# Two halves of the heads for the first unit of a gated-linear-attention and maxout kernel, with q and k of a head pair laid side by side and a new planned order

## The chip, the cores and the metric

The kernel runs on one core of a Trainium2 chip. The metric is the device time of the whole program in microseconds; the kernel before has a median of 138.03 us over 5 runs (137.97 to 138.18).

## What is computed

The attention part is a recurrence over 768 time steps for each of 4 batches and 8 heads of width 48; its output feeds a maxout block.

```python
for t in range(S):                                   # S = 768, D = 48
    state = alpha[:, :, t, :, None] * state + einsum('bhd,bhe->bhde', k[:, :, t], v[:, :, t])
    y[:, :, t] = einsum('bhd,bhde->bhe', q[:, :, t], state)
x = y.transpose(0, 2, 1, 3).reshape(B * S, H * D)    # 3072 x 384
h1, h2 = x @ w1, x @ w2                              # 384 x 1024 each
out = maximum(h1, h2) @ w_out                        # 1024 x 384
```

All inputs and the output are float32; the kernel computes with 16-bit operands and 32-bit sums.

## The kernel before: how the work is tiled and ordered

**Units and chunks.** The 3072 rows are cut into 12 units of 256 time steps (a batch and one of three positions in it), and each unit into two chunks of 128. `gla(u)` does the attention of unit u, `moe(u)` its maxout. Units 0, 1 and 2 (the tuple `TWO`) hold two neighbouring time steps in each partition, so their loads have longer runs; the branch for them is called `by2` in the code.

**One unit of attention.** ScalarE takes the logarithm of alpha (L481), TensorE sums it along time (L503 for the first three units, L492 for the others), and ScalarE takes the exponentials of the sums with both signs: `em` (L530) and, in place in the bank, the factor for q (L532). `prep(i)` then multiplies k by `em` into `kn` (L573) and q by the factor into `qn` (L575), transposes both on TensorE (L583, four head pairs each into one bank), and copies the transposed pair out: into `qu` for the first three units (L588), into `qk` for the others (L593). `chunk(a)` makes P, the products of transposed k and q (L676); VectorE multiplies P by a triangular mask into `pt` (L698); TensorE adds up the output from `pt` and v (L710) and from the carried state and q (L707); ScalarE copies it to `yc` (L718); TensorE transposes it (L724) and VectorE copies the result to `xt` (L732, L735). The carried state goes through k times v (L604 or L647), a sum `tm` (L659, L661, L663) and a scaled copy `sb` on GpSimd (L634). GpSimd or VectorE also lays v out as 16 bits (`vx`, L556; the other half rows by ScalarE, L560).

**The maxout.** max(h1, h2) is written as x·w2 + relu(x·(w1 − w2)). So the kernel needs w1 − w2 in four pieces of 256 columns (`w12`, a VectorE subtraction, L460), w_out in 16 bits in four pieces (`wo16`, L465), and the product w2·w_out (`w2o`): w2 is cast (L432), transposed (L440), copied (L444) and multiplied by `wo16` (L450, 24 matmuls, six for each piece of w_out). `moe(u)` then has eight half-pairs: four products `hp` with one piece of `w12` each (L765, six matmuls), each followed by a relu on ScalarE (L776), and two output sums `op` (L796) that begin with the three matmuls on `w2o` and go on through the four pieces in order. ScalarE copies them out (L804) and issues the store (L812).

**What sets the order.** Nothing is ordered by the program text alone. Every step is entered with `add(engine, function, duration, reads, writes, key)`; a list scheduler (`Plan.schedule`) plays the engines forward with these durations and, on each engine, picks the ready step with the smallest key. Keys are 10·u plus an offset: 0 to 4.5 inside `gla(u)`, `KEY_M` and more inside `moe(u)`, `KEY_W`, `KEY_W12` and `KEY_WO` for the weights. The dictionary `PRI` shifts keys of single steps. The engines' instruction streams are then written in the planned order and each engine runs its own stream in order. Where the plan leaves TensorE idle in its first 40 us, `busy` puts matmuls on a constant tile there (L471). The first loads are issued by SyncE in the order of `HEAD`, in which `a0` is alpha of unit 0 and so on, `w20` to `w22` are the row blocks of w2, `w10` to `w13` the column pieces of w1, and `wo0` to `wo3` the pieces of w_out.

The lines that set the engine of single steps are these:

```python
KEY_W12 = 8; KEY_W = 3; KEY_WO = 21; KEY_M = 20
WT_ACT = (0,)       # w2T copies on ScalarE, the others on VectorE
WO_ACT = (2, 3)     # casts of w_out pieces on ScalarE, the others on GpSimd
TM_ACT = 2          # units whose first tm goes through ScalarE
QU_ACT = (1,)       # chunks whose qu copy is on ScalarE
KN_DVE = (0,); VX_DVE = (0,)   # chunks whose kn, vx are on VectorE, the others on GpSimd
HEAD = 'a0 a1 k0 q0 v0 q1 k1 w20 w22 v1 w21 wo0 wo1 wo2 w13 w10 wo3 w11 w12'
```

Of the kernel before, what the change touches and what calls it, by code (L numbers as in the profile page):

```python
# [7 lines left out]
FP16 = mybir.dt.float16  # L8
# [177 lines left out]

KEY_W12 = 8
KEY_W = 3
KEY_WO = 21
KEY_M = 20  # L190
CAPS = {'g': 6, 'm': 5, 'w': 3}
W12_POOL = ()
WT_ACT = (0,)
WO_ACT = (2, 3)
RELU_DVE = 99
TM_ACT = 2
X_LAST = 0
# [3 lines left out]
TWO = (0, 1, 2)  # L201
MERGE = 3
COMBO = 99
JOIN_CS = -2
JOIN_PP = -50
CS_UP = 2
RING = 3
# [3 lines left out]
XT_ACT = ()  # L211
QU_ACT = (1,)
KN_DVE = (0,)
VX_DVE = (0,)
PRI = {'PE:op.1.1.0@1': 10, 'PE:op.0.0.0@0': 15.0, 'PE:op.1.0.0@1': 3, 'PE:op.0.1.0@0': 4.5, 'DVE:tm.4.1@3': -33.5, "POOL:('vx', 2).1@2": -16.5, 'PE:hp.1.1@1': -3.0, 'PE:cs.4.0@4': -10, 'POOL:kn.1@6': -5, 'POOL:sb.0.0@4': 12, 'PE:hp.3.3@3': 1.5, 'ACT:qu.0.1@0': -13.5, 'PE:hp.4.1@4': 5.0, 'DVE:pt.1.1@5': 5, 'PE:pp.0.1.0@0': -15, 'DVE:pt.0.0@0': 9, 'PE:y.5.0@5': 10.5, 'PE:hp.5.1@5': 13.5, 'DVE:tm.2.1@3': -9, 'ACT:cs.7.0@7': 5, 'PE:op.4.1.0@4': 9, 'DVE:tm.2.1@4': -11, 'PE:y.0.0@0': 5, 'DVE:pt.0.1@3': 10, 'PE:cs.2.0@2': -9, 'DVE:tm.3.1@5': 9, 'ACT:cs.7.1@7': -5, 'PE:hp.2.3@2': -3, 'PE:pp.1.0.0@1': 3}
HEAD = 'a0 a1 k0 q0 v0 q1 k1 w20 w22 v1 w21 wo0 wo1 wo2 w13 w10 wo3 w11 w12'


@with_exitstack
def kernel(  # L220
# [53 lines left out]
    VX = sbt("vx", [128, 3, H, D], FP16, max(1, len(TWO)))  # L274
    QU = sbt("qu", [128, 2, 2, HP, 2, 64], FP16, 2)
    w2f, w1f = (LD[i].rearrange("p a x -> p (a x)").rearrange("p (s f) -> p s f", s=ND) for i in (4, 5))
# [18 lines left out]
    def two(t):  # L295
        return t.rearrange("p (h r d) -> p r h d", r=2, h=H)

    P = Plan()
# [78 lines left out]
    for i in range(RING):  # L377
        add("DVE", lambda i=i: nc.vector.memset(KN[i][:, :, D:64], 0.0), 0.17, writes=[("kn", i)], key=-6)
        add("DVE", lambda i=i: nc.vector.memset(QN[i][:, :, D:64], 0.0), 0.17, writes=[("qn", i)], key=-5)
    for i in range(2):  # L380
# [76 lines left out]
    def weights(g):  # L457
        fs = slice(256 * g, 256 * g + 256)
        eng, ns = ("POOL", nc.gpsimd) if g in W12_POOL else ("DVE", nc.vector)
        add(eng, lambda: ns.tensor_sub(out=w12[:, :, fs], in0=w1f[:, :, fs], in1=w2f[:, :, fs]),  # L460
            1.9 if g in W12_POOL else 0.95, reads=[("w1f", g), *(("w2f", ds) for ds in range(ND))],
            writes=[("w12", g)], key=KEY_W12)
        on = g in WO_ACT
        cp = nc.scalar.copy if on else nc.gpsimd.tensor_copy
        add("ACT" if on else "POOL", lambda: cp(  # L465
            out=wo16[:, 2 * g : 2 * g + 2, :], in_=wof[:, 2 * g : 2 * g + 2, :]),
            0.73 if on else 0.9, reads=[("wof", g)], writes=[("wo16", g)], key=KEY_W)

# [69 lines left out]
    def gla(u):  # L538
        P.u = u
        n, by2 = u % NLD, u in TWO  # L540
        k0 = 10 * u
        de, cp = DE[u % 8], u // B
# [21 lines left out]
        def prep(i):  # L564
# [7 lines left out]
            on, ns = ("DVE", nc.vector) if ci in KN_DVE else ("POOL", nc.gpsimd)  # L572
            add(on, lambda: ns.tensor_mul(out=kn[:, :, 0:D], in0=kin, in1=EM[m3]),  # L573
                0.55 if on == "DVE" else 0.97, reads=[*rk, ("em", m3)], writes=[("kn", m3)], key=kk)
            add("DVE", lambda: nc.vector.tensor_mul(out=qn[:, :, 0:D], in0=qin, in1=csv(u, i)),  # L575
                0.5, reads=[*rq, ("cs", u, i)], writes=[("qn", m3)], key=kk)
            tp = ("tp", u, i)
            P.ps(tp, 1, "g")
            for w, (src, key) in enumerate(((qn, ("qn", m3)), (kn, ("kn", m3)))):
                def e_tp(w=w, src=src):  # L580
                    t = b16(tp, 1024).rearrange("p (w j c) -> p w j c", w=2, j=HP)
                    for j in range(HP):
                        nc.tensor.transpose(t[:, w, j, :], pm(src[:, 2 * j : 2 * j + 2, :]), ident)  # L583
                add("PE", e_tp, 0.222, reads=[key, "ident"], writes=[tp], key=kk)
            if by2:
                on = ci in QU_ACT
                cp = nc.scalar.copy if on else nc.vector.tensor_copy
                add("ACT" if on else "DVE", lambda: cp(  # L588
                    out=qu[:, :, :, :, i, :].rearrange("p a w j c -> p (w j) a c"),
                    in_=b16(tp, 1024).rearrange("p (y a c) -> p y a c", a=2, c=64)),  # L590
                    1.0 if on else 0.65, reads=[tp], writes=[("qu", TWO.index(u) % 2, i)], key=kk)
            else:
                add("DVE", lambda: nc.vector.tensor_copy(  # L593
# [16 lines left out]
        def chunk(a):  # L610
# [7 lines left out]
            if by2:  # L618
                qt = [qu[:, a, w].rearrange("p j r c -> p j (r c)") for w in range(2)]
                rqk, vc, rv, um, ru = [("qu", TWO.index(u) % 2, 0), ("qu", TWO.index(u) % 2, 1)], vx[:, 2 * a], [(vk, x) for x in range(4)], u2, "u2"  # L620
            else:
# [16 lines left out]
            if more:  # L638
                if by2:
                    if a == 0:  # L640
                        P.ps(("kv", u, 1), 1, "g")
                        add("PE", kv2, 0.35, reads=[("kn", (2 * u) % RING), ("kn", (2 * u + 1) % RING), (vk, 0), (vk, 1)],
                            writes=[("kv", u, 0), ("kv", u, 1)], key=kk + 0.1, tiled=True)
                else:
                    def e_kv():
                        for j in range(HP):
# [3 lines left out]
                            )  # L650
                    add("PE", e_kv, 0.168, reads=[("kn", m3), ("vc", m4)], writes=[kvp], key=kk + 0.1)
                tmi = P.tm_next(u % B)
# [16 lines left out]

            def e_p(which):  # L670
                for w in which:
                    qt, pp, _ = qts[w]
                    for j in range(HP):
                        for e in range(2):
# [3 lines left out]
            if u < MERGE:  # L678
                add("PE", lambda: e_p((a,)), 0.215, reads=rqk, writes=pp, key=kk, tiled=True, join=kk + JOIN_PP)
            elif a == 0:  # L680
# [15 lines left out]
            uv = um.rearrange("p r c -> p (r c)") if by2 else um  # L696
            for e in range(2):
                add("DVE", lambda e=e: nc.vector.tensor_mul(  # L698
                    out=pt[:, e], in0=b32(pp[e], 512).rearrange("p (j c) -> p j c", j=HP),
                    in1=uv.unsqueeze(1).to_broadcast([128, HP, C])),  # L700
                    0.6, reads=[pp[e], ru], writes=[("pt", m3, e)], key=kk)

            def e_y():
# [10 lines left out]
            add("PE", e_y, 0.378 if has else 0.21,  # L714
                reads=[*rqk, ("pt", m3, 0), ("pt", m3, 1), *rv] + ([("sb", m4, 0), ("sb", m4, 1)] if has else []),
                writes=[yp], key=kk)
# [173 lines left out]
```

## Time and profile before

| What | Value |
|---|---|
| median of 5 runs | 138.03 us |
| the profiled execution's own time | 138.18 us |
| its span in the profile | 136.5 us, so 1.68 us lie around the span |
| TensorE busy (PE) | 131.7 us, 96% |
| VectorE (DVE), ScalarE (ACT), GpSimd (POOL) busy | 90.8, 91.1, 65.1 us |
| TensorE on the constant tile (L471) | 122 matmuls, 10.9 us busy, all before 18.8 us |
| granted TensorE clock | 1.0 in every stretch |

How to read it: PE is TensorE's matmuls and PEld its weight loads, which run beside them. Matmuls are pipelined, so a row's mean (273 ns for a 256-column product) is longer than the distance from one to the next; the chain of work that ended last shows the distances. Times in the views count from the start of the span.

### The profile page before, as it was taken

The page shows a single profiled execution, that of the slowest core. Times are in us where ns is not written, and L with a number is a line of the kernel's source. Part 1 is how long each engine was busy: PE and PEld are TensorE (multiplying, and loading weights), DVE is VectorE, ACT ScalarE, POOL GpSimd, SP SyncE. Part 2 cuts the span into 40 slices and gives each one's busy share as a digit, 9 for nine tenths or more (in the row PEclk, how much of TensorE's full clock was granted, in tenths as well). Part 3 has the DMA queues.
Part 4 walks back from the last instruction along what each step waited for, and adds up shares of the span by engine and source line. Part 5 has one row for each costly group of instructions (what it writes and reads, how often), then busy time and mean ns, then how long its engine had stood idle before and what let it go on. Part 6 is the DMA issues. An engine that isn't in the chain of part 4 may idle for free.

```text
span 136.5 us, 4240 instructions
## 1 busy us (share of the span) xinstructions
PE 131.7 (96%) x1669; PEld 102.2 (75%) x1669; DVE 90.8 (67%) x201; ACT 91.1 (67%) x189; POOL 65.1 (48%) x126
## 2 busy tenths in 40 slices
PE   6999999999999999999999999999999999999990
PEld 6898876777668777777877777777777778777870
DVE  4579897823899778967789479566758657572000
ACT  3697785899856956865846667568749468264640
POOL 7453974007594384470780773743747619300000
PEclk9999999999999999999999999999999999999999
DMA  3999999999999999979999989999979130030202
GB/s 93 323 325 389 388 371 356 294 250 261 212 218 258 265 233 196 313 154 221 296 185 248 252 202 231 207 214 285 222 172 237 37 115 0 5 115 0 102 30 104
DMA packets 84179, 28.58 MB, mean 209 GB/s; under 512 B 78400, under 2 KB 83392, under 8 KB 84160
## 3 DMA queue, kind: packets, MB, share of 16 engines
q1 hardware_dynamic: 81120, 23.60, 71.7%
q10 hardware_dynamic: 3040, 4.72, 9.5%
q8 instruction: 13, 0.21, 0.6%
q14 instruction: 6, 0.05, 0.1%
HBM read 23.59 MB, written 4.72 MB: 207 GB/s over the span
## 4 chain that ended last, share of the span: by engine, by line
PE 81%; SPq 8%; DMA 6%; ACT 1%; issue 1%; ACTq 0%
PE pb L796 31%; PE pb L765 23%; PE pb L583 7%; DMA ld<-in_moe_w_out_dram 6%; SPq L393 5%; PE pb L676 4%; SPq L421 3%; PE pb L710 3%; PE pb L724 3%; PE pb L707 2%; PE pb L492 2%; PE pb L450 2%; PE pb L647 2%; PE pb L525 1%; ACT wo L465 1%
## 5 line engine op out<-in xcount | busy, mean ns | idle before, releaser
L573 POOL TENSOR_TENSOR kn<-ld,em 128x384 f16<-128x384 f32 x23 | 22.7, 1001 | 35.5 <-ACT em L530 22.0
L796 PE MATMUL pb<-wo,gt 128*128 128x384 f16 (+2 forms) x200 | 39.2, 319 | 0.0
L765 PE MATMUL pb<-xt,w 128*128 128x256 f16 x288 | 35.6, 272 | 0.0
L698 DVE TENSOR_TENSOR pt<-pb,u 128x512 f16<-128x512 f32 x48 | 30.1, 683 | 6.2 <-PE pb L676 5.7
L776 ACT ACTIVATE gt<-pb 128x512 f16<-128x512 f32 x48 | 28.3, 599 | 8.4 <-PE pb L765 7.5
L765 PEld LDWEIGHTS <-w 128*128 128x128 f16 x288 | 27.0, 98 | 4.4 <-issue 0.6
L634 POOL TENSOR_TENSOR sb<-tm,dd 64x192 f16<-64x192 f32 x40 | 20.3, 506 | 11.3 <-DVE tm L659 5.1
L796 PEld LDWEIGHTS <-gt 128*128 128x128 f16 x200 | 17.4, 97 | 8.2 <-issue 0.3
L804 ACT COPY os<-pb 128x384 f32<-128x384 f32 (+2 forms) x25 | 11.7, 467 | 16.7 <-PE pb L796 16.7
L593 DVE COPY qk<-pb 128x1024 f16<-128x1024 f16 x18 | 12.4, 689 | 7.2 <-PE pb L583 7.1
L575 DVE TENSOR_TENSOR qn<-ld,pb 128x384 f16<-128x384 f32 x24 | 12.6, 548 | 6.9 <-ACT pb L532 4.9
L796 PE MATMUL pb<-w2o,xt 128*128 128x384 f16 (+2 forms) x75 | 15.8, 319 | 0.0
L718 ACT CAST yc<-pb 128x384 f16<-128x384 f32 x24 | 11.7, 489 | 5.4 <-PE pb L710 5.4
L530 ACT ACTIVATE em<-pb 128x384 f32<-128x384 f32 x24 | 11.2, 489 | 3.9 <-PE pb L492 2.6
L659 DVE TENSOR_TENSOR tm<-pb,sb 64x192 f32<-64x192 f32 x32 | 11.3, 353 | 1.0 <-PE pb L647 0.2
L471 PE MATMUL pb<-wsrc 128*128 128x128 f16 x122 | 10.9, 251 | 1.1 <-DVE wsrc L313 1.1
L481 ACT ACTIVATE lg<-ld 128x768 f16<-128x768 f32 x12 | 10.1, 845 | 2.5 <-DMA ld<-in_alpha_dram 2.5
L532 ACT ACTIVATE pb<-pb 128x384 f32<-128x384 f32 x24 | 11.0, 486 | 0.0
L710 PEld LDWEIGHTS <-pt 128*128 128x128 f16 x192 | 9.7, 96 | 1.3
L471 PEld LDWEIGHTS <-wsrc 128*128 128x128 f16 x122 | 9.1, 115 | 1.1 <-DVE wsrc L313 1.0
L596 POOL CAST vc<-ld 128x384 f16<-128x384 f32 x18 | 9.1, 508 | 1.4 <-DMA ld<-in_v_dram 0.8
L735 DVE COPY xt<-pb 128x384 f16<-128x384 f16 x18 | 6.3, 354 | 5.2 <-PE pb L724 4.8
(86 smaller groups left out, 183.0 us busy)
## 6 DMA issues: line engine op xcount, KB each, us to landing
ld<-in_alpha_dram SPq DMA_DIRECT2D x12, 384.0 KB, 4.8
out_dram<-os ACTq DMA_DIRECT2D x11, 384.0 KB, 3.3
ld<-in_k_dram SPq DMA_DIRECT2D x18, 192.0 KB, 4.7
ld<-in_q_dram SPq DMA_DIRECT2D x18, 192.0 KB, 4.5
ld<-in_v_dram SPq DMA_DIRECT2D x18, 192.0 KB, 4.4
ld<-in_moe_w_dram SPq DMA_DIRECT2D x3, 512.0 KB, 6.6
ld<-in_moe_w_out_dram SPq DMA_DIRECT2D x4, 384.0 KB, 8.1
ld<-in_moe_w_dram SPq DMA_DIRECT2D x4, 384.0 KB, 8.8
```

Source lines behind the costliest of these rows:

```text
L471: nc.tensor.matmul(PB[b][:, 0:128], lhsT=wsrc, rhs=wsrc, start=True, stop=True)
L573: add(on, lambda: ns.tensor_mul(out=kn[:, :, 0:D], in0=kin, in1=EM[m3]), 0.55 if on == "DVE" else 0.97, reads=[*rk, ("em", m3)], writes=[( ...
L575: add("DVE", lambda: nc.vector.tensor_mul(out=qn[:, :, 0:D], in0=qin, in1=csv(u, i)), 0.5, reads=[*rq, ("cs", u, i)], writes=[("qn", m3)], ...
L593: add("DVE", lambda: nc.vector.tensor_copy(out=QK[m3], in_=b16(tp, 1024).rearrange("p (w j c) -> p w j c", w=2, j=HP)), 0.6, reads=[tp], w ...
L634: add("POOL", lambda r=r, e=e: nc.gpsimd.tensor_mul(out=sb[r, :, e], in0=TM[tmo][r], in1=dd[r, :].unsqueeze(2).to_broadcast([64, HP, D])), ...
L698: add("DVE", lambda e=e: nc.vector.tensor_mul(out=pt[:, e], in0=b32(pp[e], 512).rearrange("p (j c) -> p j c", j=HP), in1=uv.unsqueeze(1).t ...
L710: nc.tensor.matmul(t[:, 96 * j + D * e : 96 * j + D * e + D], lhsT=pt[:, e, j, :], rhs=vc[:, 2 * j + e, :], start=not has, stop=(e == 1) o ...
L718: add("ACT", lambda: nc.scalar.copy(out=yc, in_=b32(yp, DM)), 0.38, reads=[yp], writes=[("yc", ci % 2)], key=kk)
L765: nc.tensor.matmul(t[:, m, :], lhsT=w12[:, ds, f * 128 : f * 128 + 128], rhs=xt[:, ds].rearrange("p a c -> p (a c)"), start=(ds == 0), sto ...
L776: add("ACT", lambda g2=g2, v2=v2: nc.scalar.activation(out=g2, in_=v2(), func=ACTF.Relu), 0.48, reads=[x], writes=[("gt", u % 3, f2)], key ...
L796: nc.tensor.matmul(b32(x, c1 - c0), lhsT=l, rhs=r, start=first and y == 0, stop=last and y == len(ws) - 1)
L804: add("ACT", lambda m=m, x=x, c0=c0, c1=c1: nc.scalar.copy(out=os_[:, m, c0:c1], in_=b32(x, c1 - c0)), 0.06 + w / 1200.0, reads=[x], write ...
```

## The change: what it does

Six things change together.

1. A new tuple `HALF = (0,)`: for unit 0, `prep` multiplies, transposes and copies heads 0 to 3 and then heads 4 to 7, as separate steps with keys of their own, and `chunk` makes P and the masked P in two halves too. Twice as many instructions of half the width are issued for `kn`, `qn`, `qu` and `pt`; the numbers of transposes and of P matmuls stay.
2. The `qu` tile is laid out as (chunk, head pair, q or k, parity, column) in place of (chunk, q or k, head pair, parity, column), and the transposes of the first three units write their bank in the order head pair, q or k, so that one copy can take two head pairs of both.
3. Engines: `kn` of chunk 0 and `vx` of chunk 0 go from VectorE to GpSimd; the `qu` copy of chunk 1 from ScalarE to VectorE; the first `tm` of unit 1 from ScalarE to VectorE; pieces 2 and 3 of w_out from ScalarE to GpSimd; the `w2T` copy on ScalarE is block 1 and not block 0.
4. Order of the first loads: q and k of unit 0 ahead of alpha of unit 1, q0 ahead of k0; v1 ahead of w20; and behind w13 now wo3, w12, w11, w10.
5. Keys: `KEY_W12`, `KEY_W`, `KEY_M`, `JOIN_CS`, `CS_UP`.
6. `PRI` loses its 28 entries and gets one.

```diff
-KEY_W12 = 8
-KEY_W = 3
+KEY_W12 = 5
+KEY_W = 9
 KEY_WO = 21
-KEY_M = 20
+KEY_M = 18
-WT_ACT = (0,)
-WO_ACT = (2, 3)
+WT_ACT = (1,)
+WO_ACT = ()
-TM_ACT = 2
+TM_ACT = 1
-JOIN_CS = -2
+JOIN_CS = -5
-CS_UP = 2
+CS_UP = 0
-QU_ACT = (1,)
-KN_DVE = (0,)
-VX_DVE = (0,)
-PRI = {'PE:op.1.1.0@1': 10, 'PE:op.0.0.0@0': 15.0, 'PE:op.1.0.0@1': 3, 'PE:op.0.1.0@0': 4.5, 'DVE:tm.4.1@3': -33.5, "POOL:('vx', 2).1@2": -16.5, 'PE:hp.1.1@1': -3.0, 'PE:cs.4.0@4': -10, 'POOL:kn.1@6': -5, 'POOL:sb.0.0@4': 12, 'PE:hp.3.3@3': 1.5, 'ACT:qu.0.1@0': -13.5, 'PE:hp.4.1@4': 5.0, 'DVE:pt.1.1@5': 5, 'PE:pp.0.1.0@0': -15, 'DVE:pt.0.0@0': 9, 'PE:y.5.0@5': 10.5, 'PE:hp.5.1@5': 13.5, 'DVE:tm.2.1@3': -9, 'ACT:cs.7.0@7': 5, 'PE:op.4.1.0@4': 9, 'DVE:tm.2.1@4': -11, 'PE:y.0.0@0': 5, 'DVE:pt.0.1@3': 10, 'PE:cs.2.0@2': -9, 'DVE:tm.3.1@5': 9, 'ACT:cs.7.1@7': -5, 'PE:hp.2.3@2': -3, 'PE:pp.1.0.0@1': 3}
+QU_ACT = ()
+HALF = (0,)
+KN_DVE = ()
+VX_DVE = ()
+PRI = {'PE:hp.3.0@3': -9}
-HEAD = 'a0 a1 k0 q0 v0 q1 k1 w20 w22 v1 w21 wo0 wo1 wo2 w13 w10 wo3 w11 w12'
+HEAD = 'a0 q0 k0 a1 v0 q1 k1 v1 w20 w22 w21 wo0 wo1 wo2 w13 wo3 w12 w11 w10'
...
-    QU = sbt("qu", [128, 2, 2, HP, 2, 64], FP16, 2)
+    QU = sbt("qu", [128, 2, HP, 2, 2, 64], FP16, 2)
...
+        nh = 2 if u in HALF else 1
...
+            for hf in range(nh):
+                hs = slice(H // nh * hf, H // nh * (hf + 1))
+                if nh == 2:
+                    kk = k0 + 1.5 + 0.5 * i + 1.5 * hf
+                js = range(HP // nh * hf, HP // nh * (hf + 1))
...
+                add(on, lambda hs=hs: ns.tensor_mul(out=kn[:, hs, 0:D], in0=kin[:, hs], in1=EM[m3][:, hs]),
+                    0.53 if nh == 2 else 1.0 if on == "DVE" else 0.97,
+                    reads=[*rk, ("em", m3)], writes=ks, key=kk)
+                add("DVE", lambda hs=hs: nc.vector.tensor_mul(out=qn[:, hs, 0:D], in0=qin[:, hs], in1=csv(u, i)[:, hs]),
+                    0.3 if nh == 2 else 0.5, reads=[*rq, ("cs", u, i)], writes=qs, key=kk)
...
+                    add("ACT" if on_q else "DVE", lambda j0=j0, j1=j1, cp=cp: cp(
+                        out=qu[:, :, j0:j1, :, i, :].rearrange("p a j w c -> p (j w) a c"),
+                        in_=b16(tp, 1024)[:, 256 * j0 : 256 * j1].rearrange("p (y a c) -> p y a c", a=2, c=64)),
...
-                add("PE", lambda: e_p((a,)), 0.215, reads=rqk, writes=pp, key=kk, tiled=True, join=kk + JOIN_PP)
+                for hf in range(nh):
+                    js = range(HP // nh * hf, HP // nh * (hf + 1))
+                    add("PE", lambda js=js: e_p((a,), js), 0.215 / nh, reads=[x for x in rqk if nh == 1 or x[2] == hf],
+                        writes=[(*x, "h", hf) for x in pp] if nh == 2 else pp, ps=pp, key=kk, tiled=True, join=kk + JOIN_PP)
...
+            for hf in range(nh):
+                j0, j1 = HP // nh * hf, HP // nh * (hf + 1)
+                for e in range(2):
+                    add("DVE", lambda e=e, j0=j0, j1=j1: nc.vector.tensor_mul(
+                        out=pt[:, e, j0:j1], in0=b32(pp[e], 512).rearrange("p (j c) -> p j c", j=HP)[:, j0:j1],
+                        in1=uv.unsqueeze(1).to_broadcast([128, j1 - j0, C])),
+                        0.35 if nh == 2 else 0.6, reads=[(*pp[e], "h", hf) if nh == 2 else pp[e], ru], ps=[pp[e]],
```

## The prediction

> **What bounds the kernel now.** I read the page first, then the chain of work that ended last, then busy time by stretches, then the VectorE and GpSimd timelines of the head. From the page, TensorE against the others:
>
> ```profile
> PE 131.7 (96%) x1669; PEld 102.2 (75%) x1669; DVE 90.8 (67%) x201; ACT 91.1 (67%) x189; POOL 65.1 (48%) x126
> PEclk9999999999999999999999999999999999999999
> ```
>
> TensorE is the bound, at full clock. Where it starts to be shows in the chain (start, us, what):
>
> ```profile
> 12.88 8.35 DMA ld<-in_moe_w_out_dram
> 21.25 0.84 ACT wo L465
> 22.13 0.49 PE pb L450 x2
> ...
> 23.16 0.97 PE pb L450 x6
> ...
> 24.46 1.31 PE pb L765 x12
> 25.77 0.97 PE pb L450 x6
> 26.75 2.62 PE pb L765 x24
> ```
>
> Up to 22.13 the end hangs on the load stream and a cast, then on TensorE alone: 24 products in 2.62 us are 0.109 each, with no gap. The stretches say the same (length, then busy PE, PEld, DVE, ACT, POOL, clock, DMA):
>
> ```profile
> 7.42:21.40 13.98, 13.46 (x250) 11.34 (x248) 13.19 (x23) 10.74 (x23) 9.09 (x14) 1.00 1.10 369
> 24.46:34.00 9.54, 9.54 (x86) 7.41 (x84) 4.38 (x8) 8.97 (x19) 2.31 (x3) 1.00 1.04 264
> 34.00:45.00 11.00, 11.00 (x149) 8.10 (x146) 10.07 (x22) 7.85 (x17) 6.97 (x13) 1.00 1.01 229
> 45.00:125.00 80.00, 80.00 (x1035) 61.39 (x1034) 56.76 (x116) 53.36 (x116) 41.45 (x79) 1.00 0.80 186
> ```
>
> From 24.46 TensorE has no idle at all. The change leaves its work as it is, so a gain can only be more real TensorE work finished before the saturated stretch begins. In the head (7.42 to 21.40) VectorE is the full engine, 13.19 of 13.98; TensorE is filled up there with the constant tile (L471). VectorE's own timeline:
>
> ```profile
> 7.42 0.71 DVE L573 TENSOR_TENSOR kn<-ld,em 128x384 f16<-128x384 f32 x1 [1.91 <-ACT em L530]
> ...
> 12.02 1.89 DVE L698 TENSOR_TENSOR pt<-pb,u 128x512 f16<-128x512 f32 x3
> 13.82 0.73 DVE L659 TENSOR_TENSOR tm<-pb,sb 64x192 f32<-64x192 f32 x2
> ...
> 20.72 0.68 DVE L698 TENSOR_TENSOR pt<-pb,u 128x512 f16<-128x512 f32 x1
> ...
> 22.50 0.96 DVE L460 TENSOR_TENSOR w<-ld,ld 128x768 f16<-128x768 f32 x1 [0.63 <-DMA ld<-in_moe_w_out_dram]
> ```
>
> The last masked P of unit 1 ends at 21.40. At 22.50, after 0.63 idle, comes w1 − w2 of the piece w13: the view names a w_out load, but the step reads w1 and w2, and w13 is the load just due. It ends at 23.46. From a VectorE end to the matmul that waits for it the trace has 0.26 (`qu` 17.36, P 17.62). So the first product on `w12` could start at 23.72 and starts at 24.46: TensorE was still busy with L450 and the end of unit 1. These 0.74 us are all that can be gained here.
>
> **The change part by part.**
>
> *Loads.* Ahead of w13 stand the same 14 loads as before (eight of units 0 and 1, three of w2, wo0 to wo2), only permuted, and SyncE issues nothing more; w13 lands at 22.5 as before. Behind it the subtractions start at 22.50, 23.88, 25.65 and 26.78, and wo3's cast at 24.51; so wo3 now lands about 23.5, w12 24.5, w11 25.6, w10 26.8. w20 and w22 slip one place behind v1, about 1 us (w20's cast was at 14.25): covered, since the first L450 is at 20.10. alpha of unit 1 slips by two issues (1.06 and 1.15 us); its logarithm at 5.41 becomes about 7.7, while k1 was not multiplied before 13.41: covered. Unit 2's loads come behind all of these, unmoved.
>
> *TensorE.* The transposes and P matmuls are as many. P of unit 0 goes in four groups for two; a group of eight costs 0.22 in the chain beside other tiled work and 0.33 alone, so two more switches cost 0.2 us at about 10 us, where L471 fills over half of TensorE's time. Without that cover it would be 0.2 us on the path.
>
> *VectorE in the head.* What counts is the distance from start to start. Three masks take 12.02 to 13.82, 0.60 each against a row of 0.683, so an instruction gives 0.08 back to the next. Half widths are not in the trace; the nearest rows are `tm` with 192 columns, 0.353 (one operand in PSUM like the mask and `qn`), against the mask's 512 columns, 0.683: 1.03 ns a column and 0.155 fixed. So a half mask is 0.42, a half `qn` 0.35; a half `qu` (from 1024 columns 0.686, 384 columns 0.354) 0.42; less 0.08 each: 0.34, 0.27, 0.34. Unit 0 before: `kn` 0.64, two `qn` 1.16, `vx` 1.10, `qu` 0.59, four masks 2.40, together 5.89. After: four `qn` 1.08, four `qu` 1.36, eight masks 2.72, together 5.16; the first `tm` of unit 1 adds 0.70: 5.86. The same, for what it gives to GpSimd it spends on fixed costs. But it starts later: not with `kn` at 7.42, but with `qn`, whose factor (L532, from 7.29, 0.43 each) is there at 7.75. So the last mask ends near 21.40 + 0.33 = 21.7. GpSimd's four `kn` halves (0.50 each) run from 6.72 to about 9.0, but the first `qu` needs only the first, so VectorE isn't held. Bounds: without the 0.08, the eighteen new steps cost 1.44 more and the nine they replace 0.72, so 22.4 at worst; the 0.79 idle in the stretch may be used, 21.0 at best.
>
> [...]
>
> *GpSimd.* It gains `kn` of chunk 0 (1.00), `vx` (0.82) and two casts of 0.83. Up to 21.4 that is 9.09 + 1.82 of 14 us, so it has room; after 19.2 it has wo0, wo1, wo2 and wo3 as they land, and the 1.08 us of unit 1's `sb`, which before ran at 20.98:
>
> ```profile
> 20.20 0.83 POOL L465 CAST wo<-ld 128x768 f16<-128x768 f32 x1 [0.15 <-DMA ld<-in_moe_w_out_dram]
> 20.98 1.08 POOL L634 TENSOR_TENSOR sb<-tm,dd 64x192 f16<-64x192 f32 x2
> ```
>
> wo2 lands then (21.23). It doesn't collide if `sb` comes before wo0, at 18 to 19; unit 1's k is multiplied from about 11.5 (k1 landed by then, 6.58 plus 4.9) and not 13.41, so this is likely.
>
> *ScalarE* loses `qu` (1.01), `tm` (0.65) and two casts (1.67); its copy of a w2T block is moved, not added. It wasn't full: 10.74 of 13.98.
>
> *TensorE from 20.1 to 23.72.* To do: 18 L450 at 0.162, 2.92; the outputs of unit 1, 0.20 and 0.36; two transposes of `yc`, 0.33: 3.81. There is 3.62, and six of the L450 can't start before wo2's cast, about 22.2; they end at 23.2, then output and transposes. So 0.2 lands behind. Gain 0.74 − 0.20 = 0.54.
>
> *Cover behind it.* From 23.72 TensorE has w13's two products 1.31 and the last six L450 0.97, 2.28 us until 25.7, when w12's piece is ready (24.5 + 0.96 + 0.26). Each later piece brings 1.31 per 1.1 us. With the next piece late by over 0.3 us this would open a gap. Then unit 2: its `xt` ends at 42.64, usable 42.90, its product starts at 43.25 in the chain: 0.35 slack, against a TensorE 0.54 earlier. 0.19 would come back unless unit 2 itself gets quicker (its alpha sums were ready at 29.43 and ran at 30.18, behind L796). Half of it, 0.1, is taken off.
>
> *Keys and PRI.* From 45 on there is nothing to gain, as TensorE is at 80.00 of 80.00; a worse order can only open gaps. The other engines are at 52 to 71% there. I take 0, with 0 to 0.5 us of loss.
>
> Sum on the profiled execution: 138.18 − 0.54 + 0.10 = 137.74. The median lies 0.15 below that execution: 137.6 us.
>
> **The rivals.**
>
> *Nothing comes of it (chance 0.22).* Unit 0 is ready earlier, but its `xt` was there at 19.0 and waited for w12 anyway; unit 1 still ends behind 23.7. With the masks at 22.4 or later the output (0.36) and transposes (0.33) of unit 1 land behind the first product, 0.7 of TensorE's work for 0.74 us: 138.0. For it: VectorE is full and gets no relief. Against: ScalarE is freed.
>
> *Slower (0.32).* GpSimd at 21 us: all four casts and unit 1's `sb` in one queue. If `sb` comes before wo2, wo2's cast ends at 22.9 and not 22.09. TensorE's stream is in planned order, so six L450 wait in front of the first product until 23.1; they end at 24.1, then unit 1's output and transposes (0.7) and the product at 24.8 for 24.46: 0.35 lost, plus 0.1 to 0.2 of gap behind it, 138.5. The point from which it decides: `sb` of unit 1 not ready by 19.2. For it: GpSimd's `kn` and `vx` of unit 0 queue ahead of unit 1's. Against: three microseconds of its idle time before that.
>
> *All of it (0.04).* 0.74 and no loss: 137.3.
>
> **How the numbers follow.** The forecast, 137.6 (137.3 to 137.8), has 0.42. A measurement of this kernel can tell 0.2%, 0.28 us, from no change. Faster: 0.42 and 0.04, less a little for the forecast's edge, 0.44; same: 0.23; slower: 0.33. The range reaches over the rivals, with the loss of order of up to 0.5 on the same case: 137.2 to 138.7.
>
> **What would show it.** Right: the first L765 at 23.7 to 23.9; L460 first at 22.5; last mask of unit 1 by 22.2; no TensorE idle from there to the end. Wrong: L460 or the wo2 cast behind other work, L450 waiting on GpSimd, or TensorE idle near 42 us or in the last 15 us. If w13 landed at another time than 22.5, the sum fails at its first term.

## The result, and the profile after

The changed kernel is slower by a third of a per cent: median 138.49 us (137.84 to 140.89, 28 runs) against 138.05 us (137.85 to 139.48, 49 runs) of the kernel before, ratio 1.0033 with a 95% interval of 1.002 to 1.0047. Measured twice more beside other experiments, it gave 1.0035 (1.0011 to 1.0058) and 1.0014 (0.9999 to 1.003). Its fastest runs match those of before; the others spread further: the middle half lies from 138.31 to 138.65 us, that of the kernel before from 137.98 to 138.13. The forecast was 137.6, faster; 138.5 was the number of the rival "Slower".

The profiled execution took 139.33 us, at the long end of its runs; its span is 137.6 us, 1.7 around it as before. From its page:

```profile
PE 131.1 (95%) x1662; PEld 101.1 (73%) x1662; DVE 91.1 (66%) x210; ACT 88.5 (64%) x184; POOL 69.8 (51%) x132
PEclk9999999999999999999999999999999999999999
```

TensorE's work and clock are the same, so the loss is time in which it had nothing of its own to do. The busy time by stretches says where:

```profile
7.42:21.40 13.98, 12.14 (x227) 9.80 (x225) 12.20 (x31) 9.46 (x20) 10.77 (x17) 1.00 1.08 362
24.46:34.00 9.54, 9.54 (x86) 7.18 (x86) 4.70 (x9) 7.75 (x16) 2.38 (x3) 1.00 1.01 260
34.00:45.00 11.00, 11.00 (x152) 8.09 (x150) 8.47 (x19) 7.73 (x17) 6.43 (x12) 1.00 1.05 233
45.00:125.00 80.00, 80.00 (x1027) 61.39 (x1025) 58.74 (x120) 54.52 (x116) 43.15 (x82) 1.00 0.80 188
```

From 24.46 on TensorE is as full as before, and no gap has opened late. From the start of unit 2's first product (L765 before, L787 now) to the end of the last output copy it is 90.73 us before and 90.72 now: the new keys cost nothing there. All of the difference lies ahead of that product, which starts at 43.09 before and 44.24 here. The chain of work that ended last (start, us, what) shows the head:

```profile
12.42 8.36 DMA ld<-in_moe_w_out_dram
...
20.83 0.82 POOL wo L469
...
21.87 0.10 POOL wo L469
21.96 0.69 issue
22.65 0.51 POOL sb L650
...
23.23 1.18 POOL sb L650
...
24.45 0.20 PE pb L729
...
24.98 0.33 PE pb L454 x2
25.31 0.65 PE pb L787 x6
```

Before, the chain came out of the load stream by one cast on ScalarE and was on TensorE from 22.13. Now it goes on through GpSimd until 24.41: w_out casts, then unit 1's `sb`, of which the second half takes 1.18 and the first 0.51. TensorE's in-order stream waits with unit 1's output (L729), and the first product on `w12` comes behind that. GpSimd's own timeline, and below it two lines of VectorE's:

```profile
19.80 0.82 POOL L469 CAST wo<-ld 128x768 f16<-128x768 f32 x1 [1.09 <-DMA ld<-in_moe_w_out_dram]
20.83 0.82 POOL L469 CAST wo<-ld 128x768 f16<-128x768 f32 x1 [0.20 <-DMA ld<-in_moe_w_out_dram]
21.87 0.82 POOL L469 CAST wo<-ld 128x768 f16<-128x768 f32 x1 [0.22 <-DMA ld<-in_moe_w_out_dram]
22.65 1.75 POOL L650 TENSOR_TENSOR sb<-tm,dd 64x192 f16<-64x192 f32 x2
```

```profile
20.63 0.73 DVE L679 COPY tm<-pb 64x192 f32<-64x192 f32 x2
...
23.07 0.96 DVE L464 TENSOR_TENSOR w<-ld,ld 128x768 f16<-128x768 f32 x1 [0.40 <-DMA ld<-in_moe_w_dram]
```

Two things differ from the forecast's picture. The loads are late: the w_out pieces are cast at 19.80, 20.83 and 21.87 (19.22 and 20.20 before, and 21.25 on ScalarE), w13's subtraction starts at 23.07 and not at 22.50. And `sb` is last in GpSimd's queue: its `tm`, now on VectorE, runs at 20.63 behind a w2T copy (on ScalarE it ran at 19.55), and by then the casts stand ahead.

The changed kernel's executions scatter, though. Another one (experiment `e12_after_control`, span 136.2, 137.94 us) on the same engines:

```profile
18.82 0.82 POOL L469 CAST wo<-ld 128x768 f16<-128x768 f32 x1
19.89 0.82 POOL L469 CAST wo<-ld 128x768 f16<-128x768 f32 x1 [0.24 <-DMA ld<-in_moe_w_out_dram]
20.96 0.82 POOL L469 CAST wo<-ld 128x768 f16<-128x768 f32 x1 [0.25 <-DMA ld<-in_moe_w_out_dram]
21.74 1.08 POOL L650 TENSOR_TENSOR sb<-tm,dd 64x192 f16<-64x192 f32 x2
```

```profile
21.23 1.29 DVE L719 TENSOR_TENSOR pt<-pb,u 128x512 f16<-128x512 f32 x2
22.44 1.20 DVE L464 TENSOR_TENSOR w<-ld,ld 128x768 f16<-128x768 f32 x1
```

The same stream, with the pieces 0.9 to 1.0 us earlier; the first product starts at 23.76 (25.14 in the other execution, 24.30 before), unit 2's at 42.85. The profile of `e1_again` (span 137.6) repeats the late picture: casts at 19.87, 20.89 and 21.93, w13's subtraction at 23.10, first product at 25.17. In these three profiles, the landing of the loads separates the short execution from the two long ones. The profiles of other kernels with the same new load order agree: in four (e2, e5, e9, e11) w13's subtraction starts by 22.51 and the span is 136.4 or 136.6; in e7 it starts at 22.98, after a wait, and the span is 137.1.

The new order of the computation hardly wins anything even in e12's short execution. Unit 2's product is 0.24 earlier than in the profile of before, but that execution (span 136.5) is longer than the usual 136.3. Against the profile of `e16_layout_only` (span 136.3, every engine's order as before, w13's subtraction at 22.38, first product at 24.15, unit 2's at 42.94) it is 0.09 earlier.

### The profile page after: what moved, and what is told of

Same layout as the page of the kernel before. It is cut to its first block, busy times and chain, and to the rows that moved or that the text cites. A ratio compares the mean times of both kernels' runs of the same rounds, so it can differ in the third digit from the quotient of the medians.

```text
span 137.6 us, 4204 instructions
## 1 busy us (share of the span) xinstructions
PE 131.1 (95%) x1662; PEld 101.1 (73%) x1662; DVE 91.1 (66%) x210; ACT 88.5 (64%) x184; POOL 69.8 (51%) x132
## 4 chain that ended last, share of the span: by engine, by line
PE 80%; SPq 8%; DMA 6%; POOL 2%; issue 1%; ACT 0%; ACTq 0%; POOLq 0%
PE pb L818 31%; PE pb L787 23%; PE pb L597 6%; DMA ld<-in_moe_w_out_dram 6%; SPq L397 6%; PE pb L692 4%; PE pb L732 3%; PE pb L746 3%; PE pb L729 3%; PE pb L496 2%; SPq L425 2%; PE pb L663 2%; POOL sb L650 1%; PE pb L529 1%; PE pb L454 1%
## 5 line engine op out<-in xcount | busy, mean ns | idle before, releaser
L587 POOL TENSOR_TENSOR kn<-ld,em 128x384 f16<-128x384 f32 (+1 forms) x26 | 24.0, 937 | 33.9 <-ACT em L534 27.3
L818 PE MATMUL pb<-wo,gt 128*128 128x384 f16 (+2 forms) x200 | 38.2, 319 | 0.0
L787 PE MATMUL pb<-xt,w 128*128 128x256 f16 x288 | 35.9, 273 | 0.0
L719 DVE TENSOR_TENSOR pt<-pb,u 128x512 f16<-128x512 f32 (+1 forms) x52 | 30.3, 641 | 6.2 <-PE pb L692 5.9
L787 PEld LDWEIGHTS <-w 128*128 128x128 f16 x288 | 26.7, 98 | 4.8 <-issue 1.3
L650 POOL TENSOR_TENSOR sb<-tm,dd 64x192 f16<-64x192 f32 x40 | 21.1, 527 | 11.7 <-DVE tm L675 6.0
L590 DVE TENSOR_TENSOR qn<-ld,pb 128x384 f16<-128x384 f32 (+1 forms) x26 | 13.0, 518 | 9.2 <-ACT pb L536 8.6
L536 ACT ACTIVATE pb<-pb 128x384 f32<-128x384 f32 x24 | 11.6, 492 | 0.0
L475 PE MATMUL pb<-wsrc 128*128 128x128 f16 x115 | 10.4, 251 | 1.1 <-DVE wsrc L317 1.1
L597 PE MATMUL pb<-ident,kn 128*128 128x128 f16 x96 | 9.4, 219 | 1.0 <-POOL kn L587 1.0
L475 PEld LDWEIGHTS <-wsrc 128*128 128x128 f16 x115 | 8.6, 115 | 1.2 <-DVE wsrc L317 1.0
```

The costliest lines, as they stand in the source:

```text
L475: nc.tensor.matmul(PB[b][:, 0:128], lhsT=wsrc, rhs=wsrc, start=True, stop=True)
L536: add("ACT", lambda i=i: nc.scalar.activation(out=csv(u, i), in_=csv(u, i), func=ACTF.Exp), 0.38, writes=[("cs", u, i)], key=k0 + 1 + i)
L587: add(on, lambda hs=hs: ns.tensor_mul(out=kn[:, hs, 0:D], in0=kin[:, hs], in1=EM[m3][:, hs]), 0.53 if nh == 2 else 1.0 if on == "DVE" else ...
L590: add("DVE", lambda hs=hs: nc.vector.tensor_mul(out=qn[:, hs, 0:D], in0=qin[:, hs], in1=csv(u, i)[:, hs]), 0.3 if nh == 2 else 0.5, reads= ...
L650: add("POOL", lambda r=r, e=e: nc.gpsimd.tensor_mul(out=sb[r, :, e], in0=TM[tmo][r], in1=dd[r, :].unsqueeze(2).to_broadcast([64, HP, D])), ...
L719: add("DVE", lambda e=e, j0=j0, j1=j1: nc.vector.tensor_mul(out=pt[:, e, j0:j1], in0=b32(pp[e], 512).rearrange("p (j c) -> p j c", j=HP)[: ...
```

## Experiments

Outside the span lie 1.70 to 1.75 us in the kernels before and after and in most others, but 1.93 to 2.06 in the versions of the changed kernel with w_out casts moved back to ScalarE (e2, e5, e9, e11, e15) and in e6, 1.81 to 1.86 in e4 and e10. I found no cause; for these the span is the better measure. The median span is 136.3 us before and 136.7 to 136.8 after.

**e1_again, e12_after_control: the changed kernel, unchanged.**

> The changed kernel as it is, once more. In its first profile w1's last column piece (w13) landed at about 23.07, 0.57 later than before the change, the second half of unit 1's sb took 1.18 us for 0.51, and the first product with w12 started at 25.14 for 24.30 before. Queue theory (unit 1's sb stands behind the third w_out cast on GpSimd): sb again begins behind that cast and the first product starts after 24.6, whatever the landing. Load-order theory (the new order of loads makes w13 land later): w13's subtraction again begins at 23.0 or later. If it begins at 22.5 to 22.7, the late landing belonged to that one execution. Time 138.3 to 138.6.

> The changed kernel as it is, as the control of this group on the same chip. Median span 136.7 to 137.0, runs between 136.1 and 138; its profile again shows sb behind the third cast, and the second half of sb above 0.6 where the subtraction overlaps it.

138.78 us (137.77 to 140.43), ratio 1.0035, and 138.36 (137.94 to 139.04), ratio 1.0014. The loss repeats in the first; in the second it is not clear of no change. It is mostly scatter: the fastest runs match the fastest of before (137.77), the longest reach past 140.

**e2_wo2_scalar, e9_wo23_scalar: casts back on ScalarE.**

```diff
-WO_ACT = ()
+WO_ACT = (2,)
```

e9 has (2, 3), as the kernel before.

> The changed kernel with one cast, the third piece of w_out, back on ScalarE; the planned order is otherwise the same. Queue theory: sb starts right after the second cast, about 21.7, its halves take 0.51 each, unit 1's output starts by 23.0 and the first product with w12 at 24.0 to 24.4, 0.7 to 1.0 earlier than in the first profile of the change; time 137.6 to 137.9. Load-order theory: the product stays bound by w13's landing, time within 0.2 of the changed kernel, 138.2 to 138.5. If the split of unit 0 itself were the cost (fixed costs on VectorE), the time stays at 138.4 too, with unit 1's last mask as the wait that ends last.

> The changed kernel with both moved casts of w_out (third and fourth piece) back on ScalarE, planned order otherwise the same. Port theory (a GpSimd step and VectorE's subtraction of w1 and w2, two operands from SBUF, can't run side by side: in the profiles so far the second half of sb took 1.18 for 0.51, the fourth cast 1.47 for 0.83, the subtraction 1.57, 1.25 and 1.21 for 0.96 where they overlapped): nothing runs on GpSimd beside a subtraction, so all four take 0.95 to 0.96, the runs draw together and the median span is 136.3 to 136.6 against 136.8 to 137.0 of the changed kernel. Load theory (the new order of loads lands unsteadily): the runs scatter as before, median span 136.8 or more.

138.87 us, ratio 1.0047 (1.0024 to 1.0071), span 136.9; and 138.74, 1.005 (1.0034 to 1.0067), span 136.8. In the profiles the first product starts at 24.05 and 23.83: GpSimd's queue is cleared, and it gains nothing in the median; e9's runs did not draw together either. So the queue sets the path of the profiled execution above, but not the loss in the median. In e2's profile about 0.1 us of TensorE is then lost at 42 us, where the last `yc` of unit 2 stands on ScalarE behind unit 3's exponentials.

**e3_sub_after_sb: w13's subtraction held until unit 1's `sb` is written.**

```diff
+            if g == 3:
+                nc.vector.tensor_copy(out=scr, in_=SB[3][:, HP - 1, 2 * D - 2 : 2 * D])
+                nc.vector.tensor_copy(out=scr2, in_=SB[3][:, HP - 1, 0:2])
             ns.tensor_sub(out=w12[:, :, fs], in0=w1f[:, :, fs], in1=w2f[:, :, fs])
```

> The changed kernel with two tiny copies out of unit 1's sb ahead of the subtraction of w13's piece, so that VectorE's subtraction can no longer run beside GpSimd's sb. Contention theory (the subtraction reads two operands from SBUF and holds GpSimd back): both halves of sb take 0.50 to 0.53, sb ends 0.6 earlier, unit 1's output starts about 23.9; the subtraction starts only then and the first product stays near 25.0. Time 138.2 to 138.6, little changed. Without contention the second half of sb stays near 1.1 us and the product slips to 25.6 or later, 138.8 or more.

138.56 us, ratio 1.0025 (1.0004 to 1.0046). From VectorE's timeline and GpSimd's:

```profile
23.25 0.96 DVE L470 TENSOR_TENSOR w<-ld,ld 128x768 f16<-128x768 f32 x1
```

```profile
21.96 1.08 POOL L657 TENSOR_TENSOR sb<-tm,dd 64x192 f16<-64x192 f32 x2
23.43 1.47 POOL L476 CAST wo<-ld 128x768 f16<-128x768 f32 x1 [0.39 <-DMA ld<-in_moe_w_out_dram]
```

Both halves of `sb` are back at about 0.5, so the collision with the subtraction was what made one of them 1.18. But now the fourth w_out cast runs into that subtraction and takes 1.47 for 0.83. The collision is real and is moved, not removed. The first product is at 24.27 and not near 25.0 as expected; in this execution the w_out casts came earlier too (19.03, 20.13 and 21.18).

**e5_yc_first, e11_wo23_yc: e2 and e9 with that `yc` two places earlier.**

```diff
+    todo = [(de3.start - 0.001 if i == yc5.n else s, i, f) for s, i, f in todo]
```

> The kernel with the third cast back on ScalarE (e2), and in ScalarE's stream the last yc of unit 2 put two instructions earlier, ahead of unit 3's exponential and its small de, which waits for VectorE. In e2's profile TensorE's transpose of unit 2's last output waited for that yc until 42.08 and unit 2's first product came at 43.27. Wall theory (what the head gains is lost again at unit 2's output, behind unit 3's exponentials on ScalarE): yc at about 40.9 for 41.55, unit 2's first product at 42.7 to 42.9, time 0.4 less than e2, lowest runs 137.8 to 138.0. If unit 2 isn't the wall, the time stays as e2's (lowest 138.37).

> As e9, with the last yc of unit 2 ahead of unit 3's exponential on ScalarE (as in e5). Port theory: as e9, another 0.05 to 0.2 less; median span 136.2 to 136.4, no slower than before's 136.3. If the work that now lies behind the first product (a transpose and a matmul more, 0.33 us) is all that is left, the span stays 0.0 to 0.1 below before's.

138.47 us, ratio 1.0029 (1.0004 to 1.0053), span 136.5; and 138.54, 1.0036 (1.0022 to 1.0051), span 136.6. First products at 23.86 and 23.80, unit 2's at 43.03 and 42.97, hardly ahead of 43.09. e5 is 0.4 us faster than e2, as its wall theory said, but the fastest run and unit 2's product stayed behind what that theory expected. With the queue, the collision and the gap at 42 us all gone, the span is still no better than the kernel before's.

**e8_less_l450: the kernel before, with six matmuls fewer.** It leaves out a quarter of the product w2·w_out (and closes each sum two matmuls earlier), so its output is not the kernel's.

```diff
-            add("PE", lambda f=f: nc.tensor.matmul(
+            add("PE", (lambda: None) if f > 5 else lambda f=f: nc.tensor.matmul(
```

> The kernel before, in its own order, without the six L450 matmuls on the last piece of w_out (a quarter of the product of w2 and w_out is left out): 0.97 us of TensorE work taken away at 25.6 us, inside the stretch without idle. Saturation theory (the prediction's: what TensorE is spared in the head comes off the end, but for 0.2): time falls by 0.75 to 0.97, to 137.1 to 137.3. Wall theory (unit 2's output arrives at a fixed time near 42.9 set by its loads and the other engines): time falls by about the 0.35 of slack there, to 137.6 to 137.8.

137.59 us, ratio 0.997 (0.9958 to 0.9982), span 135.9. Of 0.97 us taken from TensorE 0.4 to 0.5 arrive at the end. Its profile is that of a late execution (138.12, the third w_out cast at 21.65 for 21.25); there 0.5 more is lost between 26.2 and 28.5, where the chain leaves TensorE for relus and `w2o` copies on ScalarE. The forecast's basis, less work is less time, holds here by about half.

**e10_before_casts_pool: the kernel before, with pieces 2 and 3 cast on GpSimd.**

```diff
-        cp = nc.scalar.copy if on else nc.gpsimd.tensor_copy
+        cp = nc.gpsimd.tensor_copy
```

> The kernel before, all orders as before, with only the third and fourth cast of w_out on GpSimd (in their planned places: the third between the two halves of unit 1's sb). Port and queue theory: the second half of sb ends about 22.6 and the casts fall beside subtractions; unit 1's output and the first product come 0.3 to 0.8 later, time 138.3 to 138.8, and the runs scatter like the changed kernel's. If GpSimd's queue and port don't matter: 137.9 to 138.2, tight.

138.97 us, ratio 1.0055 (1.0036 to 1.0073), span 137.1, and tight (136.7 to 137.3 in eight runs). Without the rest of the change this move costs 0.8 us of span, but doesn't bring the changed kernel's scatter, which was expected of it. So the move costs in the old order of work and, by e9, gains nothing when undone in the new one: its price belongs to the order around it.

**e7_no_half: the changed kernel without the halves.**

```diff
-HALF = (0,)
+HALF = ()
```

> The changed kernel planned anew with no unit in halves: kn, qn, qu, P and masks of unit 0 are whole, everything else as changed. If the halves help (unit 0 ready earlier, room for unit 1): 0.2 to 0.6 slower than the changed kernel, 138.7 to 139.1. If unit 0 is off the path and only VectorE's fixed costs count: 0.1 to 0.4 faster, 138.0 to 138.4. Queue theory alone: sb of unit 1 is planned between second and third cast here (tm of unit 1 planned 2 us earlier), so unit 1's output no longer waits for GpSimd.

139.0 us, ratio 1.0073 (1.0049 to 1.0098), span 137.3 (six runs), as expected if the halves help. The streams are planned anew here (`sb` comes between the second and the third cast), so it is the halves with the plan they allow that gain about 0.5 us inside the change.

**e16_layout_only: the kernel before with the new layout of q and k.**

```diff
-    QU = sbt("qu", [128, 2, 2, HP, 2, 64], FP16, 2)
+    QU = sbt("qu", [128, 2, HP, 2, 2, 64], FP16, 2)
```

> The kernel before, in its own order of everything, with only the new layout of q and k (the pairs of heads side by side in the product's output, and the transposes that read them). Every theory: nothing, 138.0 us within 0.15, span 136.3. Were the layout itself to cost, VectorE's rows at qn and qu or TensorE's transposes would be longer, and the span with them.

138.01 us, ratio 0.999 (0.998 to 1.0), span 136.3. The layout costs nothing.

**e13_before_v1_first: the kernel before with only v1 issued ahead of w20 and w22.**

The plan is still made with `HEAD`; at the end the loads are put into its slots in the order of `LOADS`:

```diff
 HEAD = 'a0 a1 k0 q0 v0 q1 k1 w20 w22 v1 w21 wo0 wo1 wo2 w13 w10 wo3 w11 w12'
+LOADS = 'a0 a1 k0 q0 v0 q1 k1 v1 w20 w22 w21 wo0 wo1 wo2 w13 w10 wo3 w11 w12'
...
+    fns = {i: P.ops[HEAD_OPS[x]].fn for i, x in zip(slots, LOADS.split())}
```

> The kernel before with every engine's order as it is; only SyncE's first loads differ: v1 is issued ahead of w20 and w22, as in the changed kernel. Theory of the loads (the changed kernel's runs scatter because eight loads with short runs of bytes stand in a row): the runs scatter as the changed kernel's do, the span's median rises from 136.3 us to 136.5-136.8, the time to 138.2-138.5, and the profile shows 300 GB/s or less in a microsecond between 10 and 13 us. Theory of the computation's order: nothing changes, span 136.3 within 0.1 and tight, time 138.0.

138.32 us (138.08 to 138.79), ratio 1.002 (1.0011 to 1.0029), span 136.6 (136.3 to 137.0). One load two places earlier costs 0.28 us with every engine's order as before; the whole change loses 0.44. The loads' theory had the median right and the scatter wrong: it stays near that of the kernel before (136.1 to 136.5 for most runs). SyncE's queue (start, us of the issues) in the kernel before, then in this one:

```profile
7.77 1.63 SPq L421 DMA_DIRECT2D ld<-in_moe_w_dram  x2
9.44 0.43 SPq L393 DMA_DIRECT2D ld<-in_v_dram  x1
9.92 1.40 SPq L421 DMA_DIRECT2D ld<-in_moe_w_dram  x1
11.36 1.99 SPq L421 DMA_DIRECT2D ld<-in_moe_w_out_dram  x3
```

```profile
7.78 1.15 SPq L394 DMA_DIRECT2D ld<-in_v_dram  x1
8.97 3.14 SPq L422 DMA_DIRECT2D ld<-in_moe_w_dram  x3
12.15 1.56 SPq L422 DMA_DIRECT2D ld<-in_moe_w_out_dram  x3
```

Behind two w2 blocks v1 takes 0.43 to issue; as the sixth q, k or v load in a row it takes 1.15. The w_out issues start 0.79 later. The data moves slower too; by single microseconds (the last column is GB/s), before and then e13:

```profile
11.00:12.00 1.00, 1.00 (x28) 0.71 (x22) 0.91 (x2) 0.98 (x3) 0.00 (x0) 1.00 1.04 410
12.00:13.00 1.00, 1.00 (x21) 0.79 (x20) 0.98 (x2) 0.67 (x3) 0.67 (x2) 1.00 1.04 422
```

```profile
11.00:12.00 1.00, 1.00 (x25) 0.69 (x21) 0.81 (x2) 0.95 (x4) 0.16 (x1) 1.00 1.17 320
12.00:13.00 1.00, 1.00 (x24) 0.90 (x19) 1.00 (x3) 0.28 (x2) 0.85 (x3) 1.00 0.99 304
```

The cast of w20 on ScalarE then starts at 15.06 for 14.25, and TensorE, whose stream has that block's transposes next, has no work at all from 15 to 16 us. Most of this is made up again: the w_out pieces are cast no later (19.27 and 20.93 for the first and third, 19.22 and 21.25 before), and the first product starts at 24.21 (24.30 before, 24.15 in e16). The loss comes behind it. The w1 pieces land later; the first subtraction starts at 22.67 (22.50 before, 22.38 in e16), the second at 24.05 (23.88 and 23.76), and the weight load of the seventh product (PEld) waits for that one:

```profile
25.07 0.44 PEld L766 LDWEIGHTS <-w 128*128 128x128 f16 x5 [0.32 <-DVE w L461]
```

The seventh product starts 0.31 behind the sixth (24.76), where the products before and after it are 0.11 apart. Unit 2's product is at 43.22, 0.28 behind e16's. That the slower data is what delays the w1 pieces is likely, but not shown apart from the issues.

**e4_old_loads, e14_after_v1_later, e15_all_fixes: the changed streams with the old loads.** e4 issues all first loads in the old order, e14 moves only v1 back behind w20 and w22, e15 is e11 with that.

The edit of e14 (the slots are filled as in e13):

```diff
 HEAD = 'a0 q0 k0 a1 v0 q1 k1 v1 w20 w22 w21 wo0 wo1 wo2 w13 wo3 w12 w11 w10'
+LOADS = 'a0 q0 k0 a1 v0 q1 k1 w20 w22 v1 w21 wo0 wo1 wo2 w13 wo3 w12 w11 w10'
```

> The changed kernel, all engines in its own planned order, only the first loads issued in the order of before. Load-order theory: w_out's pieces and w13 land about 0.5 earlier, 19.2, 20.2, 21.2 and 22.5, and the time falls by 0.4 or more to 138.0. Queue theory: sb still stands behind the third cast and the time changes only by what the casts come earlier; unit 0 is later and w10's and w12's products wait in the wrong order, so 138.3 to 139.0.

> The changed kernel with every engine's order as it is; only v1 is issued behind w20 and w22 again. Theory of the loads: the runs draw together, span median 136.2-136.5 us, time 137.9-138.2, the w_out pieces' casts start at 18.9, 19.9 and 21.0 us or earlier in the profile, first product at 23.8. Theory of the computation's order (residual on GpSimd behind the w_out casts): the scatter stays, span median 136.6-137.0, time 138.3-138.7.

> The changed kernel with the w_out casts of the third and the fourth piece on ScalarE, the last yc of unit 2 two places earlier on ScalarE, and v1 behind w20 and w22. Theory of the loads: span median 136.0-136.3 us, first product at 23.7-23.9, runs within 0.5 us of each other, time 0.2 above the usual distance if the time outside the span is 1.93 as in the other kernels with this move: 137.9-138.2. Theory of the computation's order: span median 136.6 as with the two moves alone.

141.3, 141.35 and 141.72 us; ratios 1.0212 (1.0165 to 1.0258), 1.0204 (1.0168 to 1.024), 1.0247 (1.0206 to 1.0288). Every theory missed by 3 us. ScalarE's line in e14:

```profile
16.75 0.51 ACT L566 CAST vx<-ld 64x384 f16<-64x384 f32 x1 [4.30 <-DMA ld<-in_v_dram]
```

In the changed stream ScalarE casts v1 before w20; v1 late stops ScalarE for 4.30 us and everything behind it. The stretches of e14 show what follows at TensorE:

```profile
16.00:18.00 2.00, 0.21 (x3) 0.18 (x3) 0.36 (x1) 1.20 (x3) 1.27 (x3) 0.87 1.06 391
18.00:20.00 2.00, 2.00 (x27) 2.00 (x26) 1.10 (x3) 1.92 (x4) 1.94 (x4) 0.50 1.08 364
```

It has little to do from 14 to 18 (0.86 us busy in the first two, 0.21 in the others) and then runs at a granted clock of 0.50; e15 does the same (0.90 and 0.38). But e4, with 1.23 us of work in the same four and nothing at all from 15 to 17, kept 1.00 and lost its 3 us all the same. What lowered the clock in the two is not shown. So the load order and the streams belong together: going back in one alone makes a third kernel, and these three runs say nothing on how the loss of the change divides.

**e6_first_loads_old: the old first loads, and the streams planned anew for them.**

```diff
-HEAD = 'a0 q0 k0 a1 v0 q1 k1 v1 w20 w22 w21 wo0 wo1 wo2 w13 wo3 w12 w11 w10'
+HEAD = 'a0 a1 k0 q0 v0 q1 k1 w20 w22 v1 w21 wo0 wo1 wo2 w13 wo3 w12 w11 w10'
```

> The changed kernel planned anew with the first loads in the order of before up to w13 (a0 a1 k0 q0 v0 q1 k1 w20 w22 v1 w21 and so on) and the new order behind it (wo3 w12 w11 w10). Load-order theory: the changed kernel's wide scatter (137.8 to 140.9) and the late landing in two of its profiles come from the new order of the first loads, so the runs draw together as before's do (137.9 to 138.3) and the median falls below 138.3. Queue theory: GpSimd's order is the same as in the changed kernel, sb behind the third cast, so the median stays at 138.4 or above whatever the landing.

138.77 us, ratio 1.0057 (1.0039 to 1.0075), span 136.85 (136.3 to 137.4, six runs). In the profile, the shortest of the six, the first product is at 23.97 and `sb` again stands behind the third cast (21.75); the median isn't better, and the runs don't draw together. The queue theory's number holds, the load-order theory's does not: the old load order isn't enough to save the change.

## Why the prediction was wrong, by its steps

**What bounds the kernel: right.** TensorE is full behind the first product, everything is decided before it, and the new keys cost nothing from unit 2 on.

**Loads, "w13 lands at 22.5 as before": the step that failed.** Counting the loads ahead of w13 isn't enough: their order changed what issuing one costs (v1 1.15 for 0.43 us in e13) and how fast the stream runs (320 and 304 GB/s there for 410 and 422). w13's subtraction started at 23.07 and 23.10 in two profiles, at 22.44 in a third; v1's place alone, which the sum took at zero ("covered"), is worth 0.28 us in the kernel before (e13, w13's subtraction at 22.67). The text had named this as its first term.

**GpSimd, "`sb` comes before wo0, so this is likely": failed.** k1 was multiplied at 12.70, after 1.61 us of waiting for its landing, not at 11.5 (in e12 the k loads of its size take 6.0 us from issue to landing in the median, for the 4.9 in the sum); and `tm`, moved to VectorE, came at 20.63. `sb` ran at 22.65 or 21.74, past the rival's deciding point of 19.2 in every profile. The rival named the right queue and was wrong on who loses by it: `sb` didn't hold up the third cast, it waited behind it. By e2 and e9 this queue isn't the median's cause. So the rival's 138.5 fits by luck.

**VectorE in the head: the durations right but for `qu`, the end too early.** Half masks take 0.35 each in a row (six in 2.08) for the forecast's 0.34, half `qn` 0.30 (four in 1.21) for 0.27: the rows carried. A half `qu` takes 0.42 as its row said, but two in a row take 0.87: they give nothing back to each other, where the sum had 0.34 each. But the last mask ends at 22.68 or 22.52, past the worst bound of 22.4, since the sum took VectorE as busy throughout and it waits: for unit 0's `sb` around 15 us 0.73 in the one profile and 0.99 in the other, and for TensorE before that 0.60 and 0.48 more. The forecast also missed that the subtraction and GpSimd's steps held each other up: it took 1.20 for 0.96 in e12 beside `sb`, and the `sb` half 1.18 for 0.51 beside it in the first profile.

**TensorE, 0.2 of work behind the first product: too small.** From the first product to unit 2's it is 18.79 before and 19.09 in e12, both without any idle time. Added up by line in the chain, 0.27 of the 0.3 stands at the transposes of unit 1's output: L746 has 9 for 6 (L724) and 0.61 for 0.34, 0.17 for three transposes more and 0.10 for pauses at them. The matmuls on w_out behind the first product are six as before, 0.97 (e11's expectation counts one more; there is none), and what the other lines gain and lose nearly cancels. So with the first product 0.54 earlier than in the profile of before (the forecast had 0.74, with 0.2 more behind it), unit 2's is only 0.24 earlier.

**The sum.** Where the loads come early (e12's profile, span 136.2 against 136.5 in the profile of before), 0.54 less 0.3 is a gain of 0.24 at unit 2; the forecast had 0.74 less 0.20 less 0.10, 0.44. In the profile of before w13 came late itself. Against e16's, where it came at 22.38, the first product is 0.39 earlier and unit 2's 0.09, and the fastest spans of both kernels are 136.1. So at best the change gains about nothing. The median's span is 0.4 to 0.5 over that of before. The new place of v1 costs 0.28 where it is tried alone, in the old streams; if it costs as much in the new ones, the rest is the scatter that these add to it.

**What stays open.** Why the changed kernel's executions scatter so much more than e13's. Its streams wait on landings more often (in the first profile, between 7.4 and 24.5 us, four groups of steps waited a microsecond or more for a DMA, on k, v, w2 and w_out, and two in the kernel before), so a jitter of the loads should come through; that is argued, not shown, and so is the split of the 0.5 into these two. e6, without the new first loads, scatters as well, so the load order can't be the only cause. Of the change's other parts, `tm` on VectorE and q and k ahead of unit 1's alpha were not tried alone. No version that I tried and that computes the whole output beats the kernel before.

## What to carry to other kernels

In a head that lives on one load queue, moving a load was not only a permutation (v1's issue went from 0.43 to 1.15 us in e13): look up the issue times and the bytes per microsecond of the new neighbours, and check each engine's stream for the first reader of what was moved. When a saturated engine starts earlier, count what now lies behind the start; here that took over half of the gain (0.30 of 0.54 us). Compare executions in which the loads come at the same time: a profile 0.2 us over its kernel's median made the other kernel look faster than it is. A step moved to a free engine must be looked up in that engine's queue at the time its input is ready, not by the engine's share of busy time.

## What the runs showed of the hardware

**Where a GpSimd step and a VectorE step with both operands in SBUF overlapped by 0.27 us or more, the one that started later took longer.** An `sb` half took 1.18 for 0.51 beside the subtraction; a w_out cast 1.47 (e3), 1.12 (e12) and 0.96 (e6) for 0.83; the subtraction itself 1.57 (e4), 1.25 (e6) and 1.20 (e12) for 0.96. VectorE's masks, which have one operand in PSUM, were not longer beside such GpSimd work: two take 1.29 in e2 (at 21.02, beside `sb` most of the time) and 1.29 in the first profile (at 18.82, GpSimd idle most of the time). In e12 GpSimd's half ends 0.38 after the subtraction's start and the subtraction is 0.24 longer, so a little less than the overlap is lost. Overlaps of about 0.1 with the fourth cast (first profile, e1) left the second subtraction at 0.96.

**With v1 late, TensorE's clock was lower afterwards in two runs of three:** 0.50 from 18 to 20 us in e14, after a cast on ScalarE that waited 4.30 us for v1, and in e15; in e4 it stayed at 1.00. In all three ScalarE did nothing from 14 to 16 us.

**The time to issue a load changed with what stood before it:** the same v1 took 0.43 us on SyncE's queue behind two w2 blocks and 1.15 behind five loads of its own kind (e13; 1.15 in the changed kernel too). A later issue was not always a later cast: e13's w_out issues start 0.79 later, the first piece is cast 0.05 later and the third 0.32 earlier.
